# Attention values loaded as 128 rows of 4 KB instead of 96, with the summaries' rows written over part of them

## The chip, the core and the metric

The kernel runs on one core of a Trainium2 chip. Five engines work side by side, each through its own list of instructions in order: PE (matrix multiplication), DVE (vector), ACT (scalar functions), POOL (general), SP (which here issues the DMAs). An instruction may start when the semaphores that it waits for have been raised, and whatever stands behind it on the same engine waits with it. The metric is the device time of one execution in microseconds (us), lower is better.

## What is computed

```python
def _attn_ref(q, k, v):                      # q, k, v: (4, 8, 768, 64)
    block, window = (32, 16)
    k_sum = k.reshape(B, H, nb, block, D).max(axis=3)     # 24 summaries a head
    v_sum = v.reshape(B, H, nb, block, D).mean(axis=3)
    scores_l = where(|i - j| < window, scale * q @ k.T, -1e9)
    scores_s = scale * q @ k_sum.T + log(block)
    a = softmax(concatenate([scores_l, scores_s], -1))
    return a @ concatenate([v, v_sum], axis=2)

x = attn_out as (3072, 512)
h = x @ w_in; x = (h * cos(h)) @ w_out       # w_in 512x2048, w_out 2048x512
# then soft routing: softmax of x @ phi, 32 slots, 8 experts of two matrices each
```

The window is banded, so a block of 64 queries needs only 96 keys of its neighbourhood and 24 summaries: 120 rows of values (`KC = 120`, of them `KL = 96` neighbours).

## The kernel before

Tokens go in 6 blocks of 512. A block takes 16 steps, one for each 128 columns of the hidden layer: step s makes `h` from `xh`, `xl` (attention output, split in a high and a low part) and `wih`, `wil` (the weight, split alike), 12 matmuls of 512 columns (`mm1`, L382 to L384). DVE and ACT turn `h` into `a` (L398, L399, the cosine on ACT at L400, then the product at L405), ACT and POOL split it into `gh`, `gl`, and two steps later 12 matmuls add it to `acc` (`mm2`, L421 to L423). There are two buffers of `h` and two of `a`: step s + 2 can't write `h` until L405 of step s has read it.

Attention is done in 24 groups, g = 0 to 23, four for each block of 512. A group's values lie in a tile `v` of 120 partitions: `load_v` (L219) brings 96 rows of 4 KB by DMA, `load_vs` fills rows 96 to 119 with the summaries, on ACT as copies for the first four groups (L225) and as two DMAs from the tile `vs` after that (L229). `att_D` (L351) multiplies by them, which gives `av`, and ACT and DVE split `av` into `xh` (L360) and `xl` (L361).

During the first block the weights arrive too: 16 loads of 1 MB (`raw`, L116), each turned into a float32 tile `w` by ACT (L125, L126), DVE (L134, L135) and POOL (L141). Two buffers of `raw` alternate, so the load of weight f + 2 waits for L135 of weight f. Keys for the summaries (`kr`, L165) come through the same queue and are reduced on DVE (`ks`, L170). The exponentials of the first eight groups (`S`, L270 and L316) run on ACT, which has to load a table each time that it goes from exponential to cosine and back.

The order in which an engine gets its instructions is set twice: `PRE` lists the tokens of the time before the first step (V = load_v, X = load_vs, S and P = the constants `sel` and `phis`, W = load_w, s, e, t, d = the parts of attention), `at2` puts the later ones at half steps; then the scheduler of the framework, by its own model of times, moves instructions of each engine's list where dependencies let it. All DMAs are issued by SP, one after the other; eight semaphores take turns among them.

Of the kernel before, what the change touches and what calls it, by code (L numbers as in the profile page):

```python
# [10 lines left out]
F32 = mybir.dt.float32  # L11
# [8 lines left out]
B, H, S, D = 4, 8, 768, 64  # L20
# [3 lines left out]
QB = 64  # L24
NQ = S // QB
WIN, SUMB = 16, 32
KL = QB + 2 * WIN
NSUM = S // SUMB
KC = KL + NSUM
# [10 lines left out]
EE = mybir.EngineType  # L40
MAN = None
PD = 1
PRE = "F I K0 Q0 M K1 Q2 W0 K2 Q1 K3 A B0 Q3 B1 B2 V0 V2 W1 V1 V3 W2 m k0 k1 s0 e0 s2 e2 k2 k3 v X0 X2 X1 X3 s1 t0 e1 s3 t2 e3 d0 t1 d2 t3 d1 d3 c0 G4 G5 W3 c1 W4 c2 w0 c3 W5 a4 a5 f V4 X4 V5 X5 S P"
NACT = 0
NABS = 0
S1 = 1
# [8 lines left out]
OV = 3  # L55
# [20 lines left out]
def body(ctx: ExitStack, tc: tile.TileContext, q0, qk, kT, vn, vx, w, phi, ex, cst, out):  # L76
    nc = tc.nc
# [66 lines left out]
    ksums, vsums, grp = {}, {}, {}  # L144
# [3 lines left out]
    def bank(name):  # L148

        pool, tag = banks[turns[0] % len(banks)]  # L150
        turns[0] += 1
        return pool.tile([128, 512], F32, name=name, tag=tag)
# [44 lines left out]
    def vsum_first():  # L197

        ps = bank("vs0")
        for i in range(3):  # L200
            vsum_mm(ps, 0, i, i == 0, i == 2)
        vsums[0] = m2.tile([128, 4, 128], F32, name="vs0", tag="sacc")
        for p in range(4):
            nc.vector.tensor_copy(vsums[0][KL:KL + 32, p, :], ps[32 * p:32 * p + 32, 0:128])
# [10 lines left out]

    def load_v(g):
        pool, tag = {2: (wres, "w7"), 3: (att, "qk")}.get(g, (att, "v"))
        t = grp[g]["v"] = pool.tile([KC, 2, 4, 128], F32, name=f"v{g}", tag=tag)
        nc.sync.dma_start(out=t[0:KL].rearrange("p j w c -> p (j w c)"), in_=vx[g])  # L219

    def load_vs(g):
        p = 2 * (g % 2)
# [119 lines left out]
    def att_D(g):  # L342
        d = grp[g]
        ps = bank(f"av{g}") if g < 4 else ps_m.tile([128, 512], F32, name=f"av{g}", tag="m")
        for j in range(2):
            aT = d["aT", j]
            for u in range(4):
                c = 256 * j + QB * u
                for hh in range(2):
                    r = slice(64 * hh, 64 * hh + 64)  # L350
                    nc.tensor.matmul(ps[r, c:c + QB], d["v"][:, j, u, r],  # L351
                                     aT[:, 128 * u + 64 * hh:128 * u + 64 * hh + 64], start=True, stop=True)
        b, o = g // 4, 256 * ((g // 2) % 2)
        if b not in xh:
            xh[b] = xres.tile([128, 4, TB], F32R, name=f"xh{b}", tag="xh", bufs=2)
            xl[b] = xres.tile([128, 4, TB], F32R, name=f"xl{b}", tag="xl", bufs=2)
        p = 2 * (g % 2)
        ps = ps.rearrange("p (j c) -> p j c", j=2)
        hi, lo = (x[b][:, p:p + 2, o:o + 256] for x in (xh, xl))
        nc.scalar.copy(hi, ps)  # L360
        nc.vector.tensor_tensor(out=lo, in0=ps, in1=hi, op=ALU.subtract)  # L361
# [4 lines left out]
    def split_w(f, part):  # L366
        d, nm = ((wi, "wi"), (wo, "wo"))[part]
        hi = ring.tile([128, 512], F32R, name=f"{nm}h{f}", tag=nm + "h")
        lo = ring.tile([128, 512], F32R, name=f"{nm}l{f}", tag=nm + "l")
        nc.scalar.copy(hi, W[f][:, part, :])  # L370
        nc.gpsimd.tensor_tensor(out=lo, in0=W[f][:, part, :], in1=hi, op=ALU.subtract)  # L371
        d[f] = (hi, lo)
# [159 lines left out]
    def at(s, pos, fn, *a):  # L532
        bg.setdefault((s, pos), []).append((fn, a))

    def at2(h, fn, *a):
        at(max(h, 0) // 2, max(h, 0) % 2, fn, *a)
# [32 lines left out]
    def masks():  # L569
        nc.vector.tensor_single_scalar(out=ident8, in_=ident, scalar=8.0, op=ALU.mult)  # L570
        nc.scalar.copy(mask_hi, mask)
        nc.gpsimd.tensor_tensor(out=mask_lo, in0=mask, in1=mask_hi, op=ALU.subtract)

    C = lambda t, o, n: (lambda _: nc.sync.dma_start(out=t, in_=cst[:, o:o + n]))
    todo = dict(F=lambda _: fill(F0), f=lambda _: fill(NFILL), I=C(ident, NM, 128), M=C(mask.rearrange("p w c -> p (w c)"), 0, NM),
                A=C(avg, NM + 128, 52), S=C(sel, NM + 180, 288), P=lambda _: nc.sync.dma_start(out=phis.rearrange("p k s -> p (k s)"), in_=phi),
                K=load_kraw, Q=load_q_first, W=load_w, B=lambda i: load_vb(0, i), V=load_v, G=load_qk, X=load_vs,
                m=lambda _: masks(), k=ksum, s=scores, e=exps, v=lambda _: vsum_first(), t=turn, d=att_D, c=convert, c1=conv_1,
                w=lambda f: split_w(f, 0), a=att_K)
    for token in PRE.split():  # L580
        n = token.lstrip("FfIMASPKQWBVGXmksevtdcwa")
# [3 lines left out]
    for g in range(4, 24):  # L585
        h0 = HF[g // 2 % 2] + 2 * NF * (g // 4 - 1) if g > 7 else HB[g // 2 % 2]
        h = h0 + OA * (g % 2)
        if g > 5:
            at2(h - OV, load_v, g)
            at2(h - OV, load_vs, g)  # L590
            at2(h - OK, att_K, g)
        at2(h, att_A, g, 0)
        at2(h + 1, att_A, g, 1)
        if g < 8:
            at2(h + 1, att_max, g, True)
            at2(h0 + OX, att_exps, g)
        else:
            at2(h + 1, att_max, g)
            at2(h + 1, att_sub, g)
            if g % 2:  # L600
                at2(h0 + OX, att_exp, g // 2)
            at2(h0 + OS + 2 * (g % 2), att_sum, g)
        h = h0 + ON + DN * (g % 2)
        at2(h, att_norm, g, nc.gpsimd if g < 8 else None)
        at2(h + OC, att_C, g, 0)
        at2(h + OC + 1, att_C, g, 1)
        at2(h + OD, att_D, g)
        if g + 2 < 24:
            at2(h0 + OQ, load_qk, g + 2)
# [33 lines left out]

    NPRE = len([x for x in PRE.split() if x[0] == 'c'])
    for f in range(NPRE, NF):
        c = max(f - CL, 0)
# [135 lines left out]
    for g in range(2):  # L782
# [16 lines left out]
        for i in range(2):  # L799
            ps = ps_m.tile([128, 512], F32, name=f"ht{g}_{i}", tag="m")  # L800
# [10 lines left out]
    for h in range(2):  # L811
        c = slice(256 * h, 256 * h + 256)
        for g in range(2):
            yp = ps_acc.tile([128, 512], F32, name=f"yp{h}_{g}", tag=f"acc{2 * g}")[:, 0:256]
            for k in range(8):
                u = 32 + 16 * h + 8 * g + 4 * (k // 4)
# [18 lines left out]
        for i in range(NB):  # L835
            pool, tag, kw = places[(NB * h + i) % 4]
            o = pool.tile([128, 4, 256], F32, name=f"o{h}_{i}", tag=tag, **kw)
            for t in range(2):
                pool, tag = pools[turn_o % 4]
                turn_o += 1  # L840
                ps = pool.tile([128, 512], F32, name=f"op{h}_{i}_{t}", tag=tag)
# [33 lines left out]
def _layout(q, k, v, moe_w_in, moe_w_out, moe2_phi, moe2_w1, moe2_w2):  # L875
    f = np.float32

    qT = q.transpose(0, 1, 3, 2).reshape(B, 4, 128, S)
    kT = np.ascontiguousarray(k.transpose(0, 1, 3, 2)).reshape(B, 4, 128, S)
    kp = np.zeros((B, 4, 128, S + 2 * WIN), f)  # L880
    kp[..., WIN:WIN + S] = kT
    vp = np.zeros((B, 4, 2, S + 2 * WIN, D), f)
    vp[:, :, :, WIN:WIN + S] = v.reshape(B, 4, 2, S, D)

    qk = np.zeros((B, 3, 2, 128, 2, 4, QB + KC), f)
    vx = np.zeros((B, 3, 2, KL, 2, 4, 2, D), f)
    for i in range(NQ):
        w = slice(QB * i, QB * i + KL)
        c = qT[..., QB * i:QB * i + QB].reshape(B, 2, 2, 128, QB)
        qk[:, i // 4, :, :, :, i % 4, :QB] = c.transpose(0, 1, 3, 2, 4)  # L890
        qk[:, i // 4, :, :, :, i % 4, QB:QB + KL] = kp[..., w].reshape(B, 2, 2, 128, KL).transpose(0, 1, 3, 2, 4)
        vx[:, i // 4, :, :, :, i % 4] = vp[:, :, :, w].reshape(B, 2, 2, 2, KL, D).transpose(0, 1, 4, 2, 3, 5)
    w_in = moe_w_in.reshape(4, 128, NF, 128).transpose(2, 1, 0, 3).reshape(NF, 128, 512)
    w = np.concatenate([w_in, moe_w_out.reshape(NF, 128, DM)], axis=2).view(np.int64)
    phi = moe2_phi.reshape(4, 128, 32).transpose(1, 0, 2).reshape(128, 128)

    e1 = moe2_w1.reshape(2, 4, 4, 128, FF).transpose(0, 2, 1, 3, 4).reshape(32, 128, 1024)
    e2 = moe2_w2.reshape(2, 4, 2, 4, 128, 2, 256).transpose(5, 0, 2, 1, 4, 3, 6).reshape(32, 128, 1024)
    return dict(
        q0=qk[0, 0:2, :, :, :, :, :QB].reshape(4, 128, -1), qk=qk.reshape(24, 128, -1)[4:], kT=kT.reshape(NP, 128, S),  # L900
        vn=v.transpose(0, 2, 1, 3).reshape(24, 128, 512), vx=vx.reshape(24, KL, -1),
        w=w, phi=phi,
        ex=np.concatenate([e1, e2], axis=0), cst=_constants())

# [16 lines left out]
```

## Time and profile before

| | |
|---|---|
| median of 3 runs | 801.28 us (799.95 to 802.89) |
| the profiled execution's own time | 798.03 us |
| its span in the trace | 796.1 us |
| PE busy | 759.4 us, 95% |
| DVE, ACT, POOL busy | 477.1, 438.2, 448.0 us |
| bytes over the span | 98.29 MB, mean 123 GB/s |
| `v` loads | 24 of 384.0 KB |
| `v<-vs` DMAs | 40 of 48.0 KB |

The span is what the trace covers; 1.9 us of the execution lie around it. A busy share is a mean over stages that differ: the first 160 us bring the weights and start the steps, then come five blocks in which the steps run, and from about 720 us on the experts.

### The profile page before, as it was taken

How to read it: one execution, taken by the hardware profiler on the slowest of the kernel's cores; microseconds unless marked ns; L12 is line 12 of the kernel's file. 1: busy time of each engine (PE TensorE's matmuls, PEld its weight loads, DVE VectorE, ACT ScalarE, POOL GpSimd, SP SyncE). 2: the span in 40 equal slices, each digit the busy share in tenths (PEclk: the TensorE clock that was granted, in tenths of full speed). 3: DMA queues.
4: the chain of work that ended last, by engine and by line, in shares of the span. 5: the costliest groups of instructions: out<-in, count | busy, mean ns of one | idle time of the engine just before them, and what ended most of it. 6: DMA issues, size and time to landing. Idle time of an engine off the chain costs nothing.

```text
span 796.1 us, 13916 instructions
## 1 busy us (share of the span) xinstructions
PE 759.4 (95%) x5517; PEld 588.2 (74%) x5517; DVE 477.1 (60%) x683; ACT 438.2 (55%) x790; POOL 448.0 (56%) x321
## 2 busy tenths in 40 slices
PE   9986878999999999999999999999999999999994
PEld 8865656777787778877778877778787888777453
DVE  5697898447567657467367468574575343443623
ACT  4969867745547546447446456465475445633222
POOL 2575997865655755655547456547557675662000
PEclk9999999999999999999999999999999999999998
DMA  9986565012241021111220020110000842237978
GB/s 314 308 292 225 203 227 197 26 58 71 72 149 39 26 64 39 50 41 62 77 77 26 26 78 25 57 46 26 26 0 27 320 182 80 80 106 283 372 297 265
DMA packets 34672, 98.29 MB, mean 123 GB/s; under 512 B 3376, under 2 KB 13744, under 8 KB 32560
## 3 DMA queue, kind: packets, MB, share of 16 engines
q1 hardware_dynamic: 34608, 97.42, 35.5%
q8 instruction: 43, 0.70, 0.3%
q14 instruction: 21, 0.17, 0.1%
HBM read 89.15 MB, written 6.29 MB: 120 GB/s over the span
## 4 chain that ended last, share of the span: by engine, by line
PE 69%; DVE 12%; DMA 9%; ACT 7%; issue 2%; SPq 0%; ACTq 0%; DVEq 0%
PE h L382 9%; PE acc L421 9%; PE acc L423 9%; PE h L383 9%; PE acc L422 8%; PE h L384 8%; DMA kr<-in_kT_dram 4%; PE sc L284 4%; PE av L351 3%; PE yp L820 2%; DMA raw<-in_w_dram 2%; PE hp L787 2%; PE tr L333 2%; PE xt L447 2%; ACT S L316 2%
## 5 line engine op out<-in xcount | busy, mean ns | idle before, releaser
L371 POOL TENSOR_TENSOR wol<-w,woh 128x512 fp32r<-128x512 f32 x96 | 139.4, 1452 | 106.4 <-ACT woh L370 106.3
L371 POOL TENSOR_TENSOR wil<-w,wih 128x512 fp32r<-128x512 f32 x96 | 130.9, 1364 | 74.6 <-ACT wih L370 73.9
L382 PE MATMUL h<-xh,wih 128*128 128x512 f32 x384 | 155.9, 406 | 10.3 <-DVE a L405 10.3
L409 POOL TENSOR_TENSOR gl<-a,gh 128x512 fp32r<-128x512 f32 x96 | 127.8, 1331 | 64.1 <-ACT gh L408 64.1
L421 PE MATMUL acc<-woh,gh 128*128 128x512 f32 x384 | 150.1, 404 | 4.9 <-ACT gh L408 4.4
L383 PE MATMUL h<-xl,wih 128*128 128x512 f32 x384 | 152.9, 398 | 1.6 <-DVE xl L361 1.6
L384 PE MATMUL h<-xh,wil 128*128 128x512 f32 x384 | 152.4, 397 | 0.0
L422 PE MATMUL acc<-wol,gh 128*128 128x512 f32 x384 | 148.8, 395 | 0.0
L423 PE MATMUL acc<-woh,gl 128*128 128x512 f32 x384 | 146.2, 396 | 0.0
L398 DVE TENSOR_SCALAR a<-h 128x512 f32<-128x512 f32 x96 | 65.8, 685 | 95.4 <-PE h L384 89.8
L400 ACT ACTIVATE a<-a,halfpi 128x512 f32<-128x512 f32 x96 | 69.5, 724 | 86.2 <-DVE a L399 84.3
L370 ACT CAST wih<-w 128x512 fp32r<-128x512 f32 x96 | 59.5, 619 | 84.0 <-PE h L383 83.1
L405 DVE TENSOR_TENSOR a<-h,a 128x512 f32<-128x512 f32 x96 | 66.2, 689 | 65.8 <-ACT a L400 65.8
L382 PEld LDWEIGHTS h<-xh,wih 128*128 128x128 f32 x384 | 72.8, 190 | 30.0 <-DVE a L405 13.3
L421 PEld LDWEIGHTS acc<-woh,gh 128*128 128x128 f32 x384 | 72.5, 189 | 24.1 <-ACT gh L408 5.3
L383 PEld LDWEIGHTS h<-xl,wih 128*128 128x128 f32 x384 | 72.8, 190 | 16.9 <-DVE xl L361 2.2
L384 PEld LDWEIGHTS h<-xh,wil 128*128 128x128 f32 x384 | 72.8, 190 | 16.4 <-POOL w L141 0.3
L422 PEld LDWEIGHTS acc<-wol,gh 128*128 128x128 f32 x384 | 72.8, 189 | 15.7 <-issue 0.5
L423 PEld LDWEIGHTS acc<-woh,gl 128*128 128x128 f32 x384 | 71.6, 188 | 17.1 <-issue 1.4
L408 ACT CAST gh<-a 128x512 fp32r<-128x512 f32 x96 | 59.4, 619 | 31.9 <-DVE a L405 31.5
L370 ACT CAST woh<-w 128x512 fp32r<-128x512 f32 x96 | 59.3, 618 | 23.1 <-PE acc L423 21.4
L399 DVE SCALAR_TENSOR_TENSOR a<-a,h 128x512 f32<-128x512 f32 x96 | 65.7, 684 | 2.4
(138 smaller groups left out, 996.6 us busy)
## 6 DMA issues: line engine op xcount, KB each, us to landing
ex<-in_ex_dram SPq DMA_DIRECT2D x64, 512.0 KB
raw<-in_w_dram SPq DMA_DIRECT2D x16, 1024.0 KB
qk<-in_qk_dram SPq DMA_DIRECT2D x20, 736.0 KB
v<-in_vx_dram SPq DMA_DIRECT2D x24, 384.0 KB
kr<-in_kT_dram SPq DMA_DIRECT2D x16, 384.0 KB
vb<-in_vn_dram SPq DMA_DIRECT2D x12, 512.0 KB
out_dram<-o SPq DMA_DIRECT2D x12, 512.0 KB
v<-vs SPq DMA_DIRECT2D x40, 48.0 KB
```

The lines of the kernel that those rows point to most:

```text
L370: nc.scalar.copy(hi, W[f][:, part, :])
L371: nc.gpsimd.tensor_tensor(out=lo, in0=W[f][:, part, :], in1=hi, op=ALU.subtract)
L382: nc.tensor.matmul(h, hi[:, c], xh[s // NF][:, t, :], start=t == 0, stop=False)
L383: nc.tensor.matmul(h, hi[:, c], xl[s // NF][:, t, :], start=False, stop=False)
L384: nc.tensor.matmul(h, lo[:, c], xh[s // NF][:, t, :], start=False, stop=t == 3)
L398: nc.vector.tensor_scalar(out=a, in0=h, scalar1=0.25, scalar2=MAGIC, op0=ALU.add, op1=ALU.add)
L400: nc.scalar.activation(a, a, AF.Sin, bias=halfpi, scale=-TWO_PI)
L405: nc.vector.tensor_tensor(out=a, in0=h, in1=a, op=ALU.mult)
L409: nc.gpsimd.tensor_tensor(out=gl, in0=a, in1=gh, op=ALU.subtract)
L421: nc.tensor.matmul(acc[t], gh[:, c], hi, start=f == 0, stop=False)
L422: nc.tensor.matmul(acc[t], gh[:, c], lo, start=False, stop=False)
L423: nc.tensor.matmul(acc[t], gl[:, c], hi, start=False, stop=f == NF - 1)
```

## The change

The array of values in memory gets 128 rows for each group instead of 96, the last 32 of them zeros, and the tile `v` gets 128 partitions. One DMA brings all 128 rows, 512 KB. Rows 96 to 119 are then written a second time by the copies or DMAs of the summaries, as before; these now write where the load has written, so they must follow its landing. `att_D` reads the first 120 partitions. In `PRE` the summaries of groups 4 and 5 go behind the loads of `sel` and `phis`, and for later groups they are put half a step later.

```diff
-PRE = "... f V4 X4 V5 X5 S P"
+PRE = "... f V4 V5 S P X4 X5"
...
-        t = grp[g]["v"] = pool.tile([KC, 2, 4, 128], F32, name=f"v{g}", tag=tag)
-        nc.sync.dma_start(out=t[0:KL].rearrange("p j w c -> p (j w c)"), in_=vx[g])
+        t = grp[g]["v"] = pool.tile([128, 2, 4, 128], F32, name=f"v{g}", tag=tag)
+        nc.sync.dma_start(out=t.rearrange("p j w c -> p (j w c)"), in_=vx[g])
...
-                    nc.tensor.matmul(ps[r, c:c + QB], d["v"][:, j, u, r],
+                    nc.tensor.matmul(ps[r, c:c + QB], d["v"][:KC, j, u, r],
...
             at2(h - OV, load_v, g)
-            at2(h - OV, load_vs, g)
+            at2(h - OV + 1, load_vs, g)
...
-    vx = np.zeros((B, 3, 2, KL, 2, 4, 2, D), f)
+    vx = np.zeros((B, 3, 2, 128, 2, 4, 2, D), f)
...
-        vx[:, i // 4, :, :, :, i % 4] = vp[:, :, :, w].reshape(B, 2, 2, 2, KL, D).transpose(0, 1, 4, 2, 3, 5)
+        vx[:, i // 4, :, :KL, :, i % 4] = vp[:, :, :, w].reshape(B, 2, 2, 2, KL, D).transpose(0, 1, 4, 2, 3, 5)
```

The scheduler then lays out other lists. They differ in the first 165 of ACT's 673 rows, the first 152 of DVE's and the first 81 of SP's; behind these the order is the same. Three places matter for what follows.

SP, at the loads for groups 4 and 5 (`raw4` is weight 4, `kr5` the sixth block of keys). Before:

```order
L116 DMA raw3_572<-in_w_dram 128x2048
L219 DMA v4_667<-in_vx_dram 96x1024
L229 DMA v4_667<-vs0_298 24x4x128
L116 DMA raw4_581<-in_w_dram 128x2048
L229 DMA v4_667<-vs0_298 24x4x128
L165 DMA kr5_765<-in_kT_dram 128x768
L219 DMA v5_671<-in_vx_dram 96x1024
```

And in the changed kernel:

```order
L116 DMA raw3_572<-in_w_dram 128x2048
L219 DMA v4_667<-in_vx_dram 128x1024
L116 DMA raw4_581<-in_w_dram 128x2048
L165 DMA kr5_765<-in_kT_dram 128x768
L229 DMA v4_667<-vs0_298 24x4x128 x2
L219 DMA v5_669<-in_vx_dram 128x1024
```

The two summary DMAs of group 4 have moved behind the weight and the keys.

DVE, at the conversion of weight 7 (`w7`) and the sums of group 5 (`sm5`, which wait for that group's exponentials on ACT). Before:

```order
L134 TENSOR_SCALAR w7_957<-w7_957 128x1024
L399 SCALAR_TENSOR_TENSOR a2_857<-a2_857,h2_836 128x512
L135 SCALAR_TENSOR_TENSOR w7_957<-raw7_827,w7_957 128x1024
L323 TENSOR_SCALAR sm5_809<-sm5_809 128x8
L325 RECIPROCAL rs5_1032<-sm5_809 128x8
```

And in the changed kernel:

```order
L399 SCALAR_TENSOR_TENSOR a2_857<-a2_857,h2_836 128x512
L323 TENSOR_SCALAR sm5_809<-sm5_809 128x8
L325 RECIPROCAL rs5_1032<-sm5_809 128x8
L134 TENSOR_SCALAR w7_957<-w7_957 128x1024
L135 SCALAR_TENSOR_TENSOR w7_957<-raw7_827,w7_957 128x1024
```

The conversion has gone behind the sums.

ACT, at the cosine of step 7 (`a7`, L400) and the exponentials of group 6 (`S6`). Before:

```order
L126 ACTIVATE cv14_1472<-raw14_1326 128x1024
L370 CAST wih9_1305<-w9_1110 128x512
L316 ACT_TABLE_LOAD
L316 ACTIVATE S6_1239,sm6_1451<-S6_1239,mx6_1286 128x120 x5
L370 CAST wih10_1360<-w10_1184 128x512
L316 ACTIVATE S6_1239,sm6_1451<-S6_1239,mx6_1286 128x120 x3
L400 ACT_TABLE_LOAD
L400 ACTIVATE a7_1233<-a7_1233,halfpi_90 128x512
```

And in the changed kernel:

```order
L400 ACTIVATE a7_1233<-a7_1233,halfpi_90 128x512
L126 ACTIVATE cv14_1472<-raw14_1326 128x1024
L370 CAST woh7_1307<-w7_957 128x512
L316 ACT_TABLE_LOAD
L316 ACTIVATE S6_1239,sm6_1451<-S6_1239,mx6_1286 128x120 x6
L408 CAST gh7_1260<-a7_1233 128x512
L316 ACTIVATE S6_1239,sm6_1451<-S6_1239,mx6_1286 128x120 x2
```

The cosine of step 7 now stands ahead of the table load and of group 6's exponentials, without a table load of its own between.

## Rows read from the trace of the kernel before

**Rows 1.** The page: the span, and 40 equal slices of it.

```profile
span 796.1 us, 13916 instructions
...
PE   9986878999999999999999999999999999999994
...
DMA  9986565012241021111220020110000842237978
```

**Rows 2.** Windows of two stages: us, busy us of each engine, PEclk, DMA share, GB/s.

```profile
0.00:160.00 160.00, 138.89 (x1202) 109.67 (x1204) 119.90 (x144) 118.65 (x262) 112.77 (x71) 0.97 0.66 223
160.00:270.00 110.00, 109.16 (x761) 86.53 (x762) 71.22 (x101) 58.41 (x96) 65.15 (x47) 1.00 0.22 70
```

**Rows 3.** Windows around the first value loads, and one of 128-row loads of 4 KB.

```profile
6.00:16.00 10.00, 10.00 (x148) 8.33 (x148) 4.96 (x9) 4.96 (x16) 1.72 (x1) 1.00 1.02 388
...
17.00:20.00 3.00, 3.00 (x50) 2.53 (x50) 3.00 (x4) 1.48 (x8) 2.29 (x1) 1.00 1.07 274
...
23.00:27.00 4.00, 4.00 (x68) 3.30 (x62) 3.85 (x7) 3.81 (x4) 3.97 (x3) 1.00 1.02 274
...
626.00:636.00 10.00, 10.00 (x45) 8.12 (x44) 4.14 (x6) 4.62 (x8) 6.59 (x7) 1.00 1.03 411
```

**Rows 4.** The chain that ended last, early part: start, length, what.

```profile
13.49 11.18 DMA v<-in_vx_dram
...
24.69 12.81 DMA kr<-in_kT_dram
```

**Rows 5.** Timeline of ACT before the first step: start, length, in brackets idle before it.

```profile
23.19 3.88 ACT L225 COPY v<-vs 24x1024 f32<-24x1024 f32 x4 [0.43 <-DVE vs L204]
...
46.01 1.17 ACT L125 ACTIVATE w<-raw 128x1024 f32<-128x1024 f32 x1 [0.81 <-DMA raw<-in_w_dram]
...
48.15 1.06 ACT L360 CAST xh<-av 128x512 fp32r<-128x512 f32 x2
...
52.73 1.14 ACT L125 ACTIVATE w<-raw 128x1024 f32<-128x1024 f32 x1 [3.52 <-DMA raw<-in_w_dram]
```

**Rows 6.** Timeline of DVE in the same stretch.

```profile
37.53 0.95 DVE L170 TENSOR_REDUCE ks<-kr 128x24 f32<-128x768 f32 x1 [2.37 <-DMA kr<-in_kT_dram]
...
52.67 1.28 DVE L361 TENSOR_TENSOR xl<-av,xh 128x512 fp32r<-128x512 f32 x2
```

**Rows 7.** Timeline of SP: a summary DMA early on, and value loads in the later blocks.

```profile
33.11 0.98 SPq L229 DMA_DIRECT2D v<-vs  x1
...
269.54 0.33 SPq L219 DMA_DIRECT2D v<-in_vx_dram  x1
...
319.91 0.33 SPq L219 DMA_DIRECT2D v<-in_vx_dram  x1
```

**Rows 8.** Timeline of DVE: end of weight 7's conversion, then the sums of group 5.

```profile
75.46 1.21 DVE L135 SCALAR_TENSOR_TENSOR w<-raw,w 128x1024 int32<-128x1024 int32 x1
78.16 1.02 DVE L323 TENSOR_SCALAR sm<-sm 128x8 f32<-128x8 f32 x1 [1.49 <-ACT S L316]
```

**Rows 9.** Timeline of ACT: table for group 6, its first exponential, the cosine of step 7.

```profile
121.39 1.28 ACT L316 ACT_TABLE_LOAD   x1
126.97 0.40 ACT L316 ACTIVATE S<-S,mx 128x120 f32<-128x120 f32 x1 [4.31 <-DVE mx L295]
...
131.95 0.72 ACT L400 ACTIVATE a<-a,halfpi 128x512 f32<-128x512 f32 x1
```

**Rows 10.** Timeline of DVE: the product (L405) of step 7 and of step 9.

```profile
132.70 0.69 DVE L405 TENSOR_TENSOR a<-h,a 128x512 f32<-128x512 f32 x1 [0.43 <-ACT a L400]
...
146.44 0.69 DVE L405 TENSOR_TENSOR a<-h,a 128x512 f32<-128x512 f32 x1 [2.14 <-ACT a L400]
```

**Rows 11.** Timeline of PE: three of its waits from 110 to 150 us.

```profile
112.42 0.50 PE L382 MATMUL h<-xh,wih 128*128 128x512 f32 x1 [2.84 <-DVE a L405]
...
133.45 0.77 PE L382 MATMUL h<-xh,wih 128*128 128x512 f32 x1 [1.79 <-DVE a L405]
146.93 0.69 PE L351 MATMUL av<-aT,v 120*64 120x64 f32 x16 [0.65 <-ACT aT L339]
```

More of the change, by code (lines that the diff above doesn't have):

```diff
@@ L42 @@
 PD = 1
-PRE = "F I K0 Q0 M K1 Q2 W0 K2 Q1 K3 A B0 Q3 B1 B2 V0 V2 W1 V1 V3 W2 m k0 k1 s0 e0 s2 e2 k2 k3 v X0 X2 X1 X3 s1 t0 e1 s3 t2 e3 d0 t1 d2 t3 d1 d3 c0 G4 G5 W3 c1 W4 c2 w0 c3 W5 a4 a5 f V4 X4 V5 X5 S P"
+PRE = "F I K0 Q0 M K1 Q2 W0 K2 Q1 K3 A B0 Q3 B1 B2 V0 V2 W1 V1 V3 W2 m k0 k1 s0 e0 s2 e2 k2 k3 v X0 X2 X1 X3 s1 t0 e1 s3 t2 e3 d0 t1 d2 t3 d1 d3 c0 G4 G5 W3 c1 W4 c2 w0 c3 W5 a4 a5 f V4 V5 S P X4 X5"
 NACT = 0
@@ L900, in _layout @@
         q0=qk[0, 0:2, :, :, :, :, :QB].reshape(4, 128, -1), qk=qk.reshape(24, 128, -1)[4:], kT=kT.reshape(NP, 128, S),
-        vn=v.transpose(0, 2, 1, 3).reshape(24, 128, 512), vx=vx.reshape(24, KL, -1),
+        vn=v.transpose(0, 2, 1, 3).reshape(24, 128, 512), vx=vx.reshape(24, 128, -1),
         w=w, phi=phi,
```

## The prediction

> **What bounds the kernel now.** I read the page's slices first. PE is at 9 tenths almost everywhere; it falls to 6 to 8 only in slices 4 to 8, that is up to 160 us, and DMA is at 9 tenths only in the first three slices and near the end [rows 1]. The windows by stage say the same with numbers: from 160 to 270 us PE is busy 109.16 of 110 us at full clock, so there only PE's work counts; before 160 us it is busy 138.89 us, so it waits 21.1 us, and its mean granted clock is 0.97 [rows 2]. What follows 160 us is the same work in the same order before and after, so the time changes by what PE waits more or less, or runs slower, in the first 160 us, and by nothing else.
>
> Within them I read the chain. Its longest early links are DMAs: values 11.18 us from issue to landing, keys 12.81 us [rows 4]. That is a queue that is full. But a link of the chain is not the price of the queue, so I looked at who waits for it. ACT, from its first summary copy at 23.19 to its last split of `av` at 48.15, waits for a DMA once, 0.81 us [rows 5]; DVE waits 2.37 us for keys [rows 6]. After the first step ACT waits 3.52 us for weight 5 [rows 5], and from there to 147 us PE waits mostly for the product L405, at the end of the loop `h`, cosine, product, next `h` [rows 11].
>
> **The loads.** Each of 24 loads grows from 384 to 512 KB, that is 131,072 bytes and 3.1 MB in all. The rate is what counts. Before the first value load the queue moves 388 GB/s; while value loads of 96 rows are in it, 274 GB/s, with the 16 engines as busy as before (share 1.07 and 1.02); the experts' loads, 128 rows of the same 4 KB, move 411 GB/s at a share of 1.03 [rows 3]. So 96 rows keep all engines busy and move less; what else is in the queue is slowed with them. Four loads lie in about 13 us from 17 on: at 274 GB/s that is 3.6 MB, with 0.5 MB more it is 4.1 MB, and at 400 GB/s (between 388 and 411) 10.2 us. The queue is some 2.8 us ahead after the first four, for a load that is a third larger.
>
> A rule of the Trainium skill can be set against this. "DMA: Bandwidth & Descriptors", section "Why a DMA increments its semaphore by 16 and not by 1", says that transfers of 128 and of 96 partitions are both split over 16 engines. Taken alone it would make a load cost by its bytes, a third more. The trace agrees on the engines (share 1.07) and not on what they then move (274 against 411 GB/s).
>
> What of the 2.8 us reaches PE? ACT does the same set of work from 23.19 to its last split of `av`, in another order, and is idle 0.81 us in it, so the splits can end at most that much earlier; DVE's 2.37 us go to work that then waits for ACT anyway (the sums of group 3). What gets shorter is the end: `xl` of the last two groups, 1.28 us on DVE [rows 6], has only one of them behind weight 4's conversion now, 0.64 us. I take **-0.5 us**, with bounds of -2.4 (all of DVE's wait) and +2.5 (below).
>
> **The summaries wait for the load.** On ACT the first copy started at 23.19, and the value load in the chain landed at 24.67 [rows 4, 5]. With the old rate that would stall ACT for the second copy (24.2) by 0.5 us, or 1.4 with 0.26 MB more at 274 GB/s. With the new rate the two loads, and the weight among them, land some 2 us sooner, before 23.2; the copies of groups 1 and 3 stand behind exponentials now. Price nothing, covered by 0.5 to 1 us; without that cover the exponentials of group 1 and all of ACT behind them are late by up to 2.5 us.
>
> On SP the DMAs of the summaries wait for a landing, and weights and keys queue behind. The SP place in the change shows that weight 4 and the keys have been put ahead of them; behind stand the load of group 5, whose buffer comes free only when `av` of group 1 is made, and weight 5, which waits for weight 3's conversion, both later than 33.11, when the first such DMA went out before [rows 7]. In later blocks a group's buffer is filled 50 us ahead of the next use of that buffer (269.54 and 319.91, rows 7); even a landing of 11.18 us [rows 4] is hidden there. Nothing.
>
> **The new order.** This is the larger term, and it isn't in the diff's numbers. Two places.
>
> DVE, group 5's sums ahead of weight 7's conversion: the conversion ended at 76.67 and the sums began at 78.16 after 1.49 us of idleness [rows 8]. Now it follows them. The exponentials come some 2.1 us earlier, as weight 7's two ACT operations have gone behind them (L125 took 1.14 in rows 5, the second much the same): sums at 76.1 to 77.1, then the conversion's two DVE operations (the second took 1.21 us, rows 8) with a POOL operation to wait for, as group 5's are made ready on POOL just then: to about 81, an estimate. That is 4.3 us later, and so is the request of weight 9. It is covered by what has moved ahead in exchange, the steps' own operations; I take **+0.5** and keep +4.3 as the bound.
>
> ACT, the cosine of step 7: before, ACT loaded the table for group 6 at 121.39, then waited 4.31 us for that group's maximum, did the eight exponentials, loaded the other table and only then, at 131.95, did the cosine of step 7 [rows 9]; its product came at 132.70 and PE, which had waited 1.79 us for it, went on at 133.45 [rows 10, 11]. Now the cosine stands ahead of that table. The idle 4.31 us began at 122.67; a cosine of 0.72 us in that place gives a product at about 124, some 8 us sooner. Step 9's product, at 146.44, also behind a table load and eight exponentials, moves ahead of group 7's in the same way. On DVE the products of steps 3, 5, 6 and 7 each stand a conversion earlier than before. So the loop runs ahead of the conversions by one weight, and the conversions keep their pace, since DVE's sum of work is the same.
>
> PE can't take 8 us of that: it takes what it waits. The three waits are 2.84, 1.79 and 0.65 us, 5.28 in all [rows 11]. With two buffers of `h` it will still stand now and then for a product; I leave it 0.3 of these and take **-5.0**. Bounds: 0 (another wait comes in their place) and -10, nearly half of the 21.1 us.
>
> **Sum.** -0.5 + 0.5 - 5.0 = -5.0 us, on the profiled execution's own 798.03 us (span 796.1 and 1.9 around it): 793.0. The median of the runs shown is 801.28, 0.4% above the profiled execution, so for a median I predict **796.3 us**, 0.6% less. A measurement of this kernel tells about 0.5%, 4 us, from no change.
>
> **The rivals.**
> *The load was off the path and the order gives nothing*: ACT's 0.81 us is all that the queue cost, and the loop, ahead in one place, is held at another (PE stands for group 6's scores or a weight's low part, which POOL makes; POOL is busy 112.77 of the first 160 us, rows 2). For it: the early chain ends in ACT and DVE, not in DMA. Against: the order moves five products forward, none back. 801.28 - 0.5 = 800.8.
> *The loads stay slow*: the rate comes from something else than the rows, and the larger load is only larger. Then the copies of the summaries hold ACT, up to 2.5 us: 803.8. Against it: 411 GB/s with the same 4 KB rows. By the rule of the Trainium skill cited above ("DMA: Bandwidth & Descriptors") the loads would go this way.
> *The conversion of weight 7 is late and stays late* (slower): DVE waits for group 5's exponentials with the conversion behind it, and weights 9, 11 and 13 follow it, each load waiting for the conversion two before. The 4.3 us are then not made up, the cosines moved ahead find their input late by as much, and the end is 801.28 + 4.3 = 805.6. It decides if weight 7's conversion ends after about 81 and weight 9's is later than before by as much. Against it: with DVE's products moved ahead of conversions there is work to fill such a wait.
>
> **How the numbers follow.** Forecast 0.55 (of it 0.07 within 0.5%), first rival 0.25, slow loads 0.07, late conversion 0.13. Faster by over 0.5%: 0.48; within: 0.07 + 0.25 + 0.07 = 0.39; slower: 0.13. The likeliest case's own range is 791 to 799: -10 is the bound, and 791 is where it would be if the step loop lost nothing at all. For 8 in 10 the range must reach over the first two rivals and leave out the third: 791 to 803.8.
>
> **What would show it.** Loads: 17 to 27 us near 400 GB/s, and no stall of ACT at the copies; a stall there and 274 GB/s speak for slow loads. Prologue: the last split of `av` within 1 us of 48.15. Loop: products of step 7 near 124 and of step 9 near 138, PE's waits from 110 to 150 down by about 5 us. Wrong if these products come early and PE waits elsewhere for the same time, or if a lower granted clock behind a longer wait eats the gain: at 133.45 the first matmul took 0.77 us where it takes 0.50 at 112.42 [rows 11].

## The result, and the profile after it

The changed kernel took **792.11 us** (median of 4 runs, 791.14 to 793.0) beside 801.01 us for the kernel before (4 runs): a ratio of 0.991, 95% interval 0.9885 to 0.9936. Measured again later beside another set of runs of before (run r12 below) it was 792.09 us and 0.9923 (0.9894 to 0.9951). The profiled execution took 791.73 us, 6.3 us less than that of before. So the gain is 6 to 9 us, with the second measurement and the trace at its lower end; the forecast was 5.

The span and the busy times on the page, and the windows of the changed kernel (columns as in [rows 1, 2]):

```profile
span 789.9 us, 13913 instructions
...
PE 759.4 (96%) x5517; PEld 586.8 (74%) x5517; DVE 473.7 (60%) x683; ACT 438.7 (56%) x790; POOL 450.4 (57%) x321
```

```profile
0.00:160.00 160.00, 144.85 (x1238) 113.19 (x1239) 117.25 (x147) 121.19 (x265) 120.42 (x74) 0.98 0.62 230
160.00:270.00 110.00, 109.13 (x754) 85.58 (x752) 72.60 (x103) 60.50 (x99) 65.19 (x48) 1.00 0.24 80
...
0.00:100.00 100.00, 88.43 (x899) 71.96 (x900) 71.10 (x95) 77.05 (x179) 61.08 (x40) 0.97 0.75 280
100.00:130.00 30.00, 27.26 (x173) 20.02 (x171) 29.23 (x31) 22.57 (x42) 30.00 (x16) 1.00 0.61 229
130.00:160.00 30.00, 29.16 (x169) 21.21 (x169) 16.91 (x22) 21.57 (x46) 29.34 (x20) 1.00 0.19 63
```

Everything happened before 160 us, as the forecast had it: PE is busy 144.85 us there, where [rows 2] had 138.89, so it waits 5.96 us less, and the span is 6.2 us shorter. Over the whole span PE is busy 759.4 us in both kernels (r12: 759.6, r2: 758.1), so the gain is waiting that has gone, not faster matmuls. The same windows of the kernel before split the 5.96 us:

```profile
0.00:100.00 100.00, 85.94 (x893) 69.96 (x894) 75.44 (x94) 75.88 (x176) 60.96 (x40) 0.98 0.80 267
100.00:130.00 30.00, 25.39 (x168) 18.86 (x168) 28.42 (x26) 18.68 (x34) 28.57 (x16) 0.94 0.67 231
130.00:160.00 30.00, 27.56 (x144) 20.86 (x144) 16.05 (x25) 24.09 (x53) 23.25 (x17) 0.94 0.19 67
```

2.5 us come before 100 us, 1.9 from 100 to 130, 1.6 behind that; it looks like a gain in three pieces. The granted clock from 100 to 160 us is 1.00 (2.4 GHz) instead of a mean of 0.94. The experiments show that the pieces are no pieces.

The loads (as [rows 3]), and ACT and DVE at the places of [rows 5, 6, 8]:

```profile
17.00:20.00 3.00, 3.00 (x54) 2.59 (x54) 2.95 (x6) 1.61 (x9) 2.35 (x1) 1.00 1.07 422
23.00:27.00 4.00, 4.00 (x64) 3.32 (x62) 3.52 (x7) 3.31 (x11) 3.57 (x3) 1.00 1.03 419
```

```profile
22.80 1.99 ACT L225 COPY v<-vs 24x1024 f32<-24x1024 f32 x2 [0.42 <-DVE vs L204]
48.55 0.59 ACT L360 CAST xh<-av 128x512 fp32r<-128x512 f32 x1
```

```profile
76.71 0.17 DVE L323 TENSOR_SCALAR sm<-sm 128x8 f32<-128x8 f32 x1 [2.77 <-ACT S L316]
...
79.64 2.20 DVE L135 SCALAR_TENSOR_TENSOR w<-raw,w 128x1024 int32<-128x1024 int32 x1
```

The rate rose from 274 to 422 GB/s at the same DMA share, and no copy of summaries on ACT waited for a landing. Yet the last split of `av` ends at 49.14 us, where the one of [rows 5] ended at 49.21: the whole prologue is no sooner. ACT's wait of 0.81 us for a weight has gone, but it now waits 0.69 us for a maximum of DVE, at 25.48. Weight 7's conversion ends at 81.8.

The loop: the cosine of step 7 on ACT, DVE's products L405 of steps 7, 8 and 9 with the conversion that stands behind step 8's, and PE's waits (as [rows 9, 10, 11]):

```profile
119.24 0.73 ACT L400 ACTIVATE a<-a,halfpi 128x512 f32<-128x512 f32 x1 [0.46 <-DVE a L399]
```

```profile
123.62 0.67 DVE L405 TENSOR_TENSOR a<-h,a 128x512 f32<-128x512 f32 x1
...
130.40 0.69 DVE L405 TENSOR_TENSOR a<-h,a 128x512 f32<-128x512 f32 x1 [0.48 <-ACT a L400]
131.43 1.13 DVE L134 TENSOR_SCALAR w<-w 128x1024 int32<-128x1024 int32 x1 [0.34 <-ACT w L125]
...
137.78 0.68 DVE L405 TENSOR_TENSOR a<-h,a 128x512 f32<-128x512 f32 x1
```

```profile
116.32 0.50 PE L382 MATMUL h<-xh,wih 128*128 128x512 f32 x1 [1.12 <-DVE a L405]
124.35 0.50 PE L382 MATMUL h<-xh,wih 128*128 128x512 f32 x1 [1.07 <-DVE a L405]
133.76 1.19 PE L423 MATMUL acc<-woh,gl 128*128 128x512 f32 x4 [0.71 <-POOL gl L409]
```

Step 7's product comes 9.1 us sooner than in [rows 10], step 9's 8.7. PE's three waits here sum to 2.90 us, those of [rows 11] to 5.28; the kernel before has a fourth wait in that stretch, which [rows 11] leave out, so the fall is 3.15 us:

```profile
125.24 0.83 PE L284 MATMUL sc<-qk 64*64 64x120 f32 x10 [0.77 <-DVE S L286]
```

What PE waited for the product, in total from 45 to 165 us, with the number of times and the longest; first the kernel before, then the changed one:

```profile
PE h L382 <- DVE a L405: 8.1, 5, 2.8
```

```profile
PE h L382 <- DVE a L405: 3.6, 3, 1.5
```

So 4.5 of the 6 us are waits for the product, from 60 us on and not only at steps 7 and 9 (r12: 4.3 us instead of 8.1).

### The profile page after: what moved, and what is told of

Same layout as the page of the kernel before. It is cut to its first block, busy times and chain, and to the rows that moved or that the text cites. A ratio compares the mean times of both kernels' runs of the same rounds, so it can differ in the third digit from the quotient of the medians.

```text
span 789.9 us, 13913 instructions
## 1 busy us (share of the span) xinstructions
PE 759.4 (96%) x5517; PEld 586.8 (74%) x5517; DVE 473.7 (60%) x683; ACT 438.7 (56%) x790; POOL 450.4 (57%) x321
## 4 chain that ended last, share of the span: by engine, by line
PE 72%; DVE 11%; ACT 10%; POOL 3%; issue 3%; DMA 1%; ACTq 0%; POOLq 0%; DVEq 0%; SPq 0%
PE h L382 9%; PE acc L421 9%; PE h L383 9%; PE h L384 9%; PE acc L423 9%; PE acc L422 9%; PE sc L284 4%; PE av L351 3%; PE yp L820 2%; PE hp L787 2%; PE tr L333 2%; PE xt L447 2%; ACT L400 1%; POOL w L141 1%; ACT S L316 1%
## 5 line engine op out<-in xcount | busy, mean ns | idle before, releaser
L371 POOL TENSOR_TENSOR wil<-w,wih 128x512 fp32r<-128x512 f32 x96 | 133.5, 1391 | 70.6 <-ACT wih L370 70.6
L400 ACT ACTIVATE a<-a,halfpi 128x512 f32<-128x512 f32 x96 | 69.5, 724 | 86.1 <-DVE a L399 85.7
L405 DVE TENSOR_TENSOR a<-h,a 128x512 f32<-128x512 f32 x96 | 66.2, 689 | 65.1 <-ACT a L400 64.8
L399 DVE SCALAR_TENSOR_TENSOR a<-a,h 128x512 f32<-128x512 f32 x96 | 65.6, 684 | 2.4
```

Of the source, the lines that this page charges most:

```text
L400: nc.scalar.activation(a, a, AF.Sin, bias=halfpi, scale=-TWO_PI)
L405: nc.vector.tensor_tensor(out=a, in0=h, in1=a, op=ALU.mult)
```

## The experiments

The change does two things at once: faster loads, and another order on all engines. The second comes wholly from the first: with 96 rows and the diff's moved calls (`X4 X5`, `h - OV + 1`) every engine has the order of before, row for row, and with 128 rows and the old calls the new one. Whether the scheduler moves things for the larger load or for its overlap with the summaries' rows isn't separated. To take rate and order apart, most runs write the whole order out, as edges to the instruction ahead on the same engine. `OLD` and `NEW` are the lists of before and of the changed kernel, and an edge sets the order of issue only:

```diff
+    for name, order in ORDER.items():
+        seq = [i for i in traced[name] if type(i).__name__ != "BassTilePoolBoundary"]
+        for a, b in zip(order, order[1:]):
+            tc.add_manual_dep(seq[b], seq[a].name, mybir.DependencyInfo(
+                mybir.DependencyClass.NoSync, mybir.DependencyReason.DATA), reason="order")
```

All runs compute the whole kernel. Ratios are to runs of before on the same chip, with the 95% interval. The median of before differs from set to set (797.8 to 801.0), so only ratios and profiled executions are compared.

| run | rows | order | us | ratio |
|---|---|---|---|---|
| r1 | 128 | old | 801.43 | 1.0033 (1.0017 to 1.005) |
| r2 | 96 | new | 792.06 | 0.9923 (0.9902 to 0.9945) |
| r3 | 96 | old, cosine 7 ahead | 798.92 | 1.0007 (0.9994 to 1.0019) |
| r4 | 112 | new | 792.38 | 0.9926 (0.9904 to 0.9948) |
| r5 | 128 | new to 58 us | 801.1 | 1.0048 (1.0032 to 1.0064) |
| r6 | 128 | new to step 2 | 800.37 | 1.0029 (1.0014 to 1.0044) |
| r7 | 128 | new to step 4 | 800.17 | 1.0022 (1.0008 to 1.0035) |
| r8 | 128 | new from step 4 | 793.82 | 0.9936 (0.9914 to 0.9959) |
| r9 | 128 | SP new, others old | 804.36 | 1.0074 (1.0053 to 1.0096) |
| r10 | 96 | new in steps 4 to 7 | 798.68 | 0.9998 (0.9979 to 1.0017) |
| r11 | 96 | new from step 8 | 798.28 | 0.9996 (0.9979 to 1.0012) |
| r12 | 128 | new (changed kernel) | 792.09 | 0.9923 (0.9894 to 0.9951) |

**Rate against order (r1, r2).** r1 is the changed kernel with `ORDER = OLD`; r2 has the load and the layout of before with `ORDER = NEW`:

```diff
-        nc.sync.dma_start(out=t.rearrange("p j w c -> p (j w c)"), in_=vx[g])
+        nc.sync.dma_start(out=t[0:KL].rearrange("p j w c -> p (j w c)"), in_=vx[g])
```

> Loads of 128 rows as in the changed kernel, but every engine takes its instructions in the order of the kernel before (the whole order written out). If the gain is the order alone: 799 to 802 us, like before. If the gain is the faster loads: 791 to 794 us, like the changed kernel. If each gives a part: between, about 796. In the trace the windows from 17 to 27 us should move near 400 GB/s in either case, since that hangs on the rows.

> Loads of 96 rows as in the kernel before, but every engine takes its instructions in the order of the changed kernel (written out). Order alone: 791 to 794 us. Loads alone: 799 to 802 us. The windows from 17 to 27 us should fall back to some 274 GB/s; if the summaries' copies then hold up the softmax of the groups behind them, as the forecast's rival of slow loads had it, ACT shows the wait at those copies and the time lies 2 to 3 us above the changed kernel.

r2 has the time of the changed kernel at the rate of before, r1 the rate of the changed kernel and a time 0.3% above before. The windows of r2:

```profile
17.00:20.00 3.00, 3.00 (x54) 2.65 (x58) 3.00 (x5) 1.48 (x8) 2.32 (x1) 1.00 1.06 266
...
23.00:27.00 4.00, 4.00 (x67) 3.32 (x62) 3.86 (x8) 3.16 (x9) 3.92 (x3) 1.00 1.01 266
```

So the order is the whole gain, and the rate is worth nothing that these intervals (some 2 us to either side) can show. The 2 to 3 us that slow loads were to cost in r2 didn't come, but r2 is no test of them: with 96 rows the summary rows don't overlap the load, so its copies on ACT (from 23.15, 30.70 and 34.33 us) had no landing to wait for. r4 below is that test. That r1 is slower than before has a place in the trace. SP in the kernel before, at group 7's load, its summary rows and the keys behind them:

```profile
112.23 0.42 SPq L219 DMA_DIRECT2D v<-in_vx_dram  x1
112.70 1.67 SPq L229 DMA_DIRECT2D v<-vs  x2
114.49 0.44 SPq L165 DMA_DIRECT2D kr<-in_kT_dram  x1
```

and in r1, with DVE and PE:

```profile
111.87 0.41 SPq L219 DMA_DIRECT2D v<-in_vx_dram  x1
118.76 1.65 SPq L229 DMA_DIRECT2D v<-vs  x2
120.52 0.45 SPq L165 DMA_DIRECT2D kr<-in_kT_dram  x1
```

```profile
123.83 0.95 DVE L170 TENSOR_REDUCE ks<-kr 128x24 f32<-128x768 f32 x1 [5.31 <-DMA kr<-in_kT_dram]
```

```profile
126.53 1.46 PE L284 MATMUL sc<-qk 64*64 64x120 f32 x10 [3.95 <-DVE S L286]
```

With 96 rows the summary rows go out at once behind the load. With 128 they overlap it and wait for its landing, 6.9 us from issue to issue; the keys wait on SP behind them, DVE behind the keys, PE behind DVE. PE's 3.95 us stand where it waited 0.77 and later 1.79 us before, so they make 1.4 of r1's 2.6 us; ACT in r1 also waits 1.23 and 0.18 us for landings at its third and fourth summary copy (25.81 and 27.03 us), and where the rest of the loss lies isn't shown. In the changed kernel the keys go out ahead of them:

```profile
113.26 0.33 SPq L165 DMA_DIRECT2D kr<-in_kT_dram  x1
113.64 1.67 SPq L229 DMA_DIRECT2D v<-vs  x2
```

In r2, where nothing overlaps, the summary rows leave in this order at 113.91: here the overlap costs nothing.

**SP's order alone (r9).** The changed kernel, with (written short here and below; the runs carry the lists themselves)

```diff
+ORDER = {e: NEW[e] if e == "SP" else OLD[e] for e in OLD}
```

> 128-row loads; SP takes its loads in the new order, the four other engines take theirs in the order of before. With 128 rows and SP's old order too, the time was 2.6 us above before, and in its trace SP sent group 7's summary rows at 118.76 instead of 112.70 us, the keys behind them at 120.52 instead of 114.49, and DVE waited 5.31 us for keys. Theory: that wait of SP for the overlapping load is the whole loss, and the new SP order, which sends the keys ahead, takes it away: equal to before within 1.5 us, DVE's wait for keys near 120 us under 2 us. Rival: the loss has another cause: 2 to 3 us above before. A third: the new SP order alone brings the gain: 6 us under before.

All three expectations fell: 0.7% slower than before. The keys are no longer what DVE waits for near 120, but weights are (ACT and DVE of r9):

```profile
123.31 1.13 ACT L125 ACTIVATE w<-raw 128x1024 f32<-128x1024 f32 x1 [4.83 <-DMA raw<-in_w_dram]
```

```profile
124.47 0.69 DVE L134 TENSOR_SCALAR w<-w 128x1024 int32<-128x1024 int32 x1 [3.83 <-ACT w L125]
```

SP sent that weight at 115.76 us, behind keys and a value load, where the kernel before sends it at 111.83, and the old order of ACT and DVE has other work queued behind it. SP's order fits one order of the others. That the overlap's wait is *all* of r1's loss isn't shown by this run, as it brings a loss of its own.

**The forecast's step by itself (r3).** The kernel before, with group 6's exponentials put behind the cosine of step 7:

```diff
-        for u in range(8):
-            nc.scalar.activation(d["S"][:, u, :], d["S"][:, u, :], AF.Exp, bias=d["mx"][:, u:u + 1],
-                                 accum_out=d["sm"][:, u:u + 1])
+        with tc.issue_after(cosine[7].ins) if g == 6 else nullcontext():
+            for u in range(8):
+                nc.scalar.activation(d["S"][:, u, :], d["S"][:, u, :], AF.Exp, bias=d["mx"][:, u:u + 1],
+                                     accum_out=d["sm"][:, u:u + 1])
...
-        nc.scalar.activation(a, a, AF.Sin, bias=halfpi, scale=-TWO_PI)
+        cosine[s] = nc.scalar.activation(a, a, AF.Sin, bias=halfpi, scale=-TWO_PI)
```

> The kernel before (96 rows) with one order changed by hand: group 6's exponentials, with their table load, come behind the cosine of step 7, as in the changed kernel; up to there the order is that of before. If the forecast's step (the cosine of step 7 ahead of the table load) carries the gain: 794 to 797 us. If the gain lies in the stretch ahead of step 7 (the rest of the new order): 799 to 802 us.

Nothing gained. This isn't one move alone: behind the edit the scheduler changed the order on DVE, PE and POOL too. ACT and PE of r3 (the lines from the edit on are one higher):

```profile
128.85 0.72 ACT L401 ACTIVATE a<-a,halfpi 128x512 f32<-128x512 f32 x1 [3.77 <-DVE a L400]
129.59 1.28 ACT L317 ACT_TABLE_LOAD   x1
```

```profile
135.10 1.82 PE L422 MATMUL acc<-woh,gh 128*128 128x512 f32 x4 [2.76 <-ACT gh L409]
```

The cosine left at 128.85, not near 123: its input, DVE's L400, stood behind a conversion and group 6's masks and maximum. Then the table and the exponentials stood behind it, `gh` of step 7 behind these, and PE waited 2.76 us for that instead of 1.79 for the product. The product itself came at 129.60, 3.1 us sooner than in [rows 10].

**Where the order pays (r5 to r8).** Each engine follows one list up to a count at which both lists have taken the same instructions, then the other; `n5` stands for r5, `n6` for r6, and `n7` for r7 and for r8, which takes `OLD` first.

```diff
+n5 = dict(ACT=70, DVE=52, PE=400, POOL=24, SP=40)
+n6 = dict(ACT=104, DVE=79, PE=478, POOL=28, SP=48)
+n7 = dict(ACT=120, DVE=94, PE=574, POOL=40, SP=50)
+ORDER = {e: NEW[e][:n[e]] + OLD[e][n[e]:] for e in n}
```

> 128-row loads; each engine takes its instructions in the new order up to about 58 us (to the fourth weight conversion after the last split of attention values), then in the order of before. Theory now: the gain lies in the loop's first twelve steps, where the new order puts a step's DVE and ACT instructions ahead of weight conversions; PE's busy time shows nothing gained by 60 us (the windows 40 to 60 us sum to 17.24 us before and 17.40 us after). Then this run equals before within 2 us. Rival: the new prologue (the copies of the summaries placed behind the softmax, other conversions) sets up all that follows; then 6 to 8 us under before.

> New order up to step 2 (about 88 us: it includes weight 7's conversion behind group 5's sums on DVE), then the order of before. By PE's busy time in the windows from 60 to 90 us (21.26 us before, 23.47 us after) the theory of a gain in pieces gives 2 us under before; the forecast's step has weight 7's late conversion as a cost of 0.5 us here. If the gain came only from the cosines of steps 7 and 9: equal to before.

> New order up to about 100 us (weights 8 to 10 converted behind the loop's steps 3 and 4, too), then the order of before. By the windows up to 100 us: 2 to 3 us under before. If everything came from what follows: equal to before.

> The complement of the run to step 4: order of before up to about 100 us, then the new order. By the windows from 100 to 160 us (52.95 us before, 56.42 us after): 3 to 4 us under before. If the parts add, its gain and that of its complement make the whole (6 to 9 us); if a step can only run ahead where the steps before it did, neither part gives its share.

By their ratios r5 to r7 lie 3.8, 2.3 and 1.8 us above before, which none of their expectations had. The mark that fits is r1, which has the same loads and the old order (1.0033), and they stay at its level: the prologue, weight 7's late conversion and steps 3 and 4 give or cost nothing that these intervals (over 1 us to either side) show. r8 has most of the gain, 1% under r1 and 5.1 us under before by its ratio. In r7 step 3's product came at 86.93 us, 5.9 us sooner than before's 92.83, and step 7's at the old time (before: 132.70, [rows 10]):

```profile
86.93 0.68 DVE L405 TENSOR_TENSOR a<-h,a 128x512 f32<-128x512 f32 x1
...
132.84 0.69 DVE L405 TENSOR_TENSOR a<-h,a 128x512 f32<-128x512 f32 x1 [0.52 <-ACT a L400]
```

A lead won before step 4 is given back where the old order stands.

**The two halves of that stretch (r10, r11).** On 96 rows, r10 takes the new order between the counts of r7 and a second set; r11 takes it behind that set only.

```diff
+n10 = dict(ACT=161, DVE=125, PE=682, POOL=54, SP=62)
+ORDER = {e: OLD[e][:n7[e]] + NEW[e][n7[e]:n10[e]] + OLD[e][n10[e]:] for e in n7}
...
+ORDER = {e: OLD[e][:n10[e]] + NEW[e][n10[e]:] for e in n10}
```

> 96-row loads as before; order of before up to about 100 us, the new order from there to about 130 us (steps 4 to 7, weights 11 to 14 converted behind the steps, the cosine of step 7 ahead of group 6's table load), order of before behind. If each stretch gains its part, the windows from 100 to 130 us (PE busy 25.39 us before, 27.26 us after) give 2 us under before. If the loop's running ahead of the conversions here carries all: 5 to 7 us. If it only pays with what follows: equal to before.

> 96-row loads as before; order of before up to about 130 us, the new order behind (the cosine of step 9 ahead of group 7's exponentials). In pieces: the windows from 130 to 160 us (PE busy 27.56 us before, 29.16 us after) give 1.6 us under before. If the stretch from step 4 to 7 carries all: equal to before.

Neither half gains anything that its interval tells from nothing. Each of the two intervals ends 1.7 us under before, so r10 leaves out its piece of 2 us and r11 alone doesn't quite leave out its 1.6. Together they give 0.5 us by their ratios, where r8, which takes both halves, gives 5.1: the theory of pieces falls, as does "steps 4 to 7 carry all". r10 shows why, on DVE and PE:

```profile
125.54 0.67 DVE L405 TENSOR_TENSOR a<-h,a 128x512 f32<-128x512 f32 x1
...
133.27 1.18 DVE L134 TENSOR_SCALAR w<-w 128x1024 int32<-128x1024 int32 x1 [1.61 <-ACT w L125]
...
134.95 2.23 DVE L135 SCALAR_TENSOR_TENSOR w<-raw,w 128x1024 int32<-128x1024 int32 x1
137.10 0.68 DVE L405 TENSOR_TENSOR a<-h,a 128x512 f32<-128x512 f32 x1
```

```profile
137.92 0.53 PE L382 MATMUL h<-xh,wih 128*128 128x512 f32 x1 [3.60 <-DVE a L405]
```

Step 7's product is 7.2 us ahead of [rows 10]. Step 8's stands in the old order behind weight 15's conversion and comes at 137.10, where the kernel before has it at 137.38, behind the same conversion:

```profile
135.71 1.75 DVE L135 SCALAR_TENSOR_TENSOR w<-raw,w 128x1024 int32<-128x1024 int32 x1
137.38 0.68 DVE L405 TENSOR_TENSOR a<-h,a 128x512 f32<-128x512 f32 x1
```

PE waits 3.60 us and the lead is gone. In the changed kernel the same product stands ahead of that conversion, at 130.40. In the kernel before the two delays, step 7's table and step 8's conversion, lie over each other in time, so removing either shows the other. r11 removes the later ones and is held by the earlier: step 8's product stands ahead of the conversion there, but waits for its cosine, which comes on ACT behind step 7's late one (r11's profiled execution was some 3.2 us late from step 0 on, so only the order and the waits are compared):

```profile
135.97 0.69 DVE L405 TENSOR_TENSOR a<-h,a 128x512 f32<-128x512 f32 x1 [0.28 <-ACT a L400]
...
140.03 0.69 DVE L405 TENSOR_TENSOR a<-h,a 128x512 f32<-128x512 f32 x1 [2.13 <-ACT a L400]
```

**The rows once more (r4), and the changed kernel again (r12).** r4 is the changed kernel in its own order, written out, with 112 rows; r12 is the changed kernel as it is.

```diff
-        nc.sync.dma_start(out=t.rearrange("p j w c -> p (j w c)"), in_=vx[g])
+        nc.sync.dma_start(out=t[0:112].rearrange("p j w c -> p (j w c)"), in_=vx[g, 0:112])
```

> Loads of 112 rows, with the order of the changed kernel. For the time, order alone: 791 to 794 us whatever the rows. For the rate of the loads: if fewer than 128 rows slow each packet, the windows from 17 to 27 us lie between 274 and 411 GB/s or stay near 274; if it were the number of bytes alone, they would be near 400.

> The changed kernel as it is, on the same chip as the partial ones. The span of the profiled execution was 6.2 us under that of before, the medians 8.9 us apart. If the span is right: 5.5 to 7 us under before; if the medians are: 8 to 10 us.

r4 has the time of the changed kernel, at this rate, and with these waits at the first two summary copies on ACT:

```profile
17.00:20.00 3.00, 3.00 (x65) 2.45 (x65) 3.00 (x6) 1.48 (x8) 2.36 (x1) 1.00 1.06 270
...
23.00:27.00 4.00, 4.00 (x64) 3.30 (x62) 3.74 (x7) 2.87 (x7) 3.77 (x3) 1.00 1.01 280
```

```profile
23.43 1.04 ACT L225 COPY v<-vs 24x1024 f32<-24x1024 f32 x1 [0.86 <-DMA v<-in_vx_dram]
25.16 1.04 ACT L225 COPY v<-vs 24x1024 f32<-24x1024 f32 x1 [0.69 <-DMA v<-in_vx_dram]
```

Its loads are slow and the summary rows overlap them: this is the stall that the forecast gave to slow loads, 1.55 us of it, and it doesn't show in the time (0.9926 beside r12's 0.9923).

r12's 0.9923 is 6.2 us of 798.81, which is the difference of the spans. r2 with its slow loads has the same ratio.

## Why the prediction was right, and where its reasons were not

- *The size:* the gain was 6.2 us (r12) for a forecast of 5.0. The forecast median, 796.3, lies 4.2 us above the measured one; 3 us of that come from 801.28, on which it was built and which stands above the later medians of before (797.8 to 798.8). That the sum comes so near is in part luck: two of its terms cancel, and the third doesn't get its size where it was looked for.
- *Where the time can change:* right. Behind 160 us PE waits 15.6 us before and 15.4 now, and PE's 5.96 us ahead of it are nearly all of the span's 6.2.
- *Loads, -0.5 us:* the rate was right (422 and 419 GB/s for an assumed 400), the price couldn't be measured: r2 has the gain without the rate. The named reason didn't come: one `xl` less stands behind weight 4's conversion, but that conversion ended 0.53 us later (53.28 for 52.75), and PE went on behind `xl` at 53.93 instead of 54.01. As it was said of ACT, the queue holds up hardly anything.
- *The summaries' wait, nothing:* in the prologue it was right that the copies need cover; with the old order they waited 1.41 us (r1), with slow loads 1.55 (r4), and r4's time shows no price for that. What the step missed sits between the prologue and the later blocks, in group 7's load at 112 us, and r1 shows it, 6.9 us on SP and 3.95 on PE. In the new order, with keys ahead, it costs nothing.
- *Weight 7's conversion, +0.5:* its end was forecast at about 81 and was 81.8. The request of weight 9 came 5.2 us later (81.91 for 76.73), but its conversion ended at 92.11, where before it ended at 92.91: the delay was made up, so the rival in which it stays late fell. r6, which has this piece, equals r1.
- *The new order, -5.0:* this term was mis-sized, and its mechanism too narrow. It measured about 6 us (r2 against before, at the old rate). It is right that the waits for the product fell; but PE's waits from 110 to 150 us fell by 3.15 us, not by 5, and the rest is spread from 60 us on. The product of step 9 came where and why it was forecast (137.78 for 138). That of step 7 came at 123.62 for "near 124" by chance: the cosine was put into ACT's idle time behind 122.67, but before, its input (DVE's L399) was made only at 128.31, and r3, which makes that move by hand, has the cosine at 128.85 and gains nothing. In the changed kernel DVE makes the input at 118.48, the cosine leaves at 119.24, and the product then stands 3.65 us on DVE behind group 6's masks and maximum and the first part of a conversion. By r3 the table is worth 3.1 us of the product's lead; that DVE's order gave the other 6 is inferred. What holds is the step's sentence that the loop runs ahead of the conversions, and it holds only as a whole from step 4 on. The rival "the loop, ahead in one place, is held at another" describes r3, r7, r10 and r11, though at other places than it named; it lost because the scheduler's order cleared the places together.
- *A lower clock after longer waits* didn't eat the gain: 100 to 160 us ran at 1.00, before at 0.94, but ahead of 100 us it was 0.97 for 0.98. PE's busy time over the span is the same, so within some 1.5 us, by which it differs between runs of one order, none of the gain is the clock's.

What stays open is which instructions beyond steps 7 and 8 have to move together; r8 falls a little short of r12 within their intervals, and so what the part before step 4 adds to it can't be told. Nor does a run tell what changing from one list to the other costs by itself in r5 to r8, r10 and r11; r9 shows that a mixture can bring a loss of its own.

## What to carry to other kernels

A change of one load's shape can act through the order that a scheduler makes of it, so write both orders out and cross them with the change before crediting the hardware. Delays that lie over each other in time don't add: a step freed at one place is worth nothing until the next step's place is freed too, so try the moves together before dropping them one by one. Rows that overlap a load put a wait on the queue that issues them; look at what stands behind it there.

## What the runs showed of the hardware

While loads of 112 rows of 4 KB were in it (r4), the DMA queue moved as little as with loads of 96: 270 and 280 GB/s, beside 274 with 96 rows (266 in r2) and 422 and 419 with 128, at a DMA share of 1.01 to 1.07 in all. So it wasn't in proportion to the rows: the full 128 moved half as much again. The expectation had left open whether 112 would lie between. What makes the difference no run here shows.
